# A long convolution's working tile: two channels of a place side by side, or eight

## The chip, the core and the metric

The kernel runs on one core of a Trainium2 chip. The core has five engines with a queue each: PE (TensorE) multiplies matrices, DVE (VectorE), ACT (ScalarE) and POOL (GpSimd) work on elements, and SP issues the DMAs. PE reads two operands from the on-chip memory: weights, which are loaded first (recorded as PEld, LDWEIGHTS), and a moving operand, which is then streamed past them (MATMUL). The metric is the time of one execution on the device in microseconds. Smaller is better.

## What is computed

A Hyena filter (a long convolution along the sequence, by FFT) is followed by a two-layer network on each token. Batch 4, sequence 12480, 128 channels, hidden width 2048:

```python
h_filt = (np.maximum(pos_emb @ w1, 0.0) @ w2) * np.exp(-0.01 * pos)[:, None]
u = x * v
Uf = np.fft.rfft(u, n=2*S, axis=1)
Hf = np.fft.rfft(h_filt, n=2*S, axis=0)
y = np.fft.irfft(Uf * Hf[None, :, :], n=2*S, axis=1)[:, :S, :]
a = (x * y).reshape(B * S, D)
h = a @ w_in
out = (h * np.cos(h)) @ w_out
```

All of it is float32.

## The kernel before

The transform of one sequence is split into two factors, N1 = 96 and N2 = 120, so that every step is a small matrix product. All steps of a batch work in place on one tile, `slots`. Its partitions are the positions of the factor that the next product sums over; along each partition it holds, before the change, 64 pairs of channels, for each pair 240 places, and for each place the two channels: `[P, 64, 240, 2]`. Two channels of a place thus lie side by side in 8 bytes, the next place of the same pair follows at once, and the same place of the next pair is 480 words (1920 bytes) further on.

A batch goes through these steps:

- **u**: x and v are loaded, multiplied (L437) and summed and subtracted into `slots` (`u_sums`, L447).
- **f1** (`f1_mm`, L455): for each pair of channels `b` and each of the two channels, two products with 64 and 60 rows of results. Here the tile is the *weights*: `u[:, b, lo:hi, i]`, one channel of 64 or 60 successive places, every second word. The table `c1` streams past it, 192 columns. The results go back to `slots` by a copy of ACT or DVE (`f1_evict`, L467), 384 words on end for each pair.
- **f2** (`f2_mm`, its products recorded at L136, the filter's at L488 and L491): for each frequency `k` the twiddled table `w` is the weights, and the tile is the *moving operand*: `parts[0:KE, :, k]`, the place `k` and its twin, of all channels, 256 columns in runs of two. The result is multiplied with the filter's spectrum `h` and put back (`f2_product`: DVE L508 and L510, POOL L511; in the first batch L504).
- **i1** (`i1_mm`, recorded at L136): as f1, with the tile as weights (96 places of one channel, 97 in the tiled part) and the table `cs` streaming, 120 columns. ACT and DVE put the results back (`i1_evict`: L531, L533; some by POOL, L527).
- **i2** (`i2_mm`, recorded at L136): for each output position the table `t` is the weights and a place of the tile is the moving operand, 128 columns in runs of two. The result is multiplied with x (L555) and stored.

The filter itself passes the same f1 and f2 once, through a tile of its own, `ftile`, and `above`, the last 48 places of `slots`. Its hidden layer lies in `aT`, a view of `above` (L387, L388), and is multiplied out by `filter_out` (L395, copies L401). While places of `slots` are free, the class `Between` lends them to the tables of sines and to five tiles of v.

The network takes the tokens in groups of 128 rows times four positions. For each group and each of 16 slices of the hidden width there is one product of 512 columns (`moe_up`, tile `ph`, later also `cv`), the cosine (L810, L811, L816, L817), sums for a Strassen scheme on POOL (L825 to L829), and a number of products of 128 columns (`moe_down`, L842, tiles `acca` and `accb`).

The order of work is written out by hand (`tc.manual_schedule`). A batch's steps are generators that yield a cost after each piece; the loop over the network's slices (98 groups of 16) lets them run for one unit of cost in each round (`convolve`), so the convolution of a batch is woven between the products of tokens that are already finished. Where the tokens run out, the convolution runs alone. From the network's start on `tiled[0]` is true: `mm` then cuts each product of the convolution and of `moe_up` into two column halves of PE (64 rows of results and the rest), which run together. The first batch's f1, f2 and i1 come before that and are not cut by `mm`; f1 cuts itself into 64 and 60 rows everywhere.

```python
    def mm(dst, left, right, start=True, stop=True):
        n = dst.shape[0]
        for lo, hi in ((0, CB), (CB, n)) if tiled[0] else ((0, n),):
            nc.tensor.matmul(dst[lo:hi], left[:, lo:hi], right, start=start, stop=stop)
```

Of the kernel before, what the change touches and what calls it, by code (L numbers as in the profile page):

```python
# [34 lines left out]
def kernel(  # L35
# [61 lines left out]
    FR = 2 * (2 * N2 - 2 * N1)  # L97
    KF = N1 - 2 * (N2 - N1)
    CB = D // 2
    assert R * N2 == S and S + TAPS - 1 <= 2 * M and math.exp(DECAY * TAPS) < 2.0 ** -150  # L100
    assert D == P and DFF % P == 0 and FO * 2 == P and N1 % 2 == 0 and R <= P
    assert NCH * ROWS <= FR <= R and H <= ODD and KE <= N1 + KF and H <= CB and N2 <= P
# [10 lines left out]
    WCOL = 256  # L113

    dram = ctx.enter_context(tc.tile_pool(name="dram", bufs=1, space=DRAM))
    hd = dram.tile([N1 // 2, N2, 2, CB, 4], F32, name="hd")
    zd = dram.tile([NROWS, G, D], F32, name="zd")
    wd = dram.tile([N1 // 2, KE, 2, N2], F32, name="wd")
    td = dram.tile([N2 // G, N1, G, 2, R], F32, name="td")
# [7 lines left out]
    c1 = const.tile([R, 3, N1], F32, name="c1")  # L127
    even = const.tile([KE, 2, N2], F32, name="even")
    tw_w = const.tile([KE, 2, N1], F32, name="tw_w")

    tiled = [False]

# [163 lines left out]
    class Between:  # L296


        def __init__(self, slots, first, last):
            self.places, self.used = slots[:, :, first:last, :], 0  # L300

        def tile(self, shape, dtype, name=None, bufs=1):
            n = 1 if len(shape) == 2 else shape[1]
            rows = self.places[0:shape[0], self.used:self.used + n].rearrange(
                "p b j i -> p b (j i)")[:, :, 0:shape[-1]]
            self.used += n
            return rows if len(shape) == 3 else rows[:, 0]

# [72 lines left out]
    def filter_hidden(bank, aT, i, peT, w1_sb):  # L381

        pa = bank()
        nc.tensor.matmul(pa[:, 0:ROWS * H], w1_sb[:, :], peT[:, :], start=True, stop=True)
        rows = slice(i * ROWS, (i + 1) * ROWS)
        pj = pa[:, 0:ROWS * H].rearrange("p (n a) -> p a n", a=H)
        nc.scalar.activation(aT[0:FO, 0:H, rows], pj[0:FO], AF.Relu)  # L387
        nc.vector.tensor_scalar(out=aT[FO:P, 0:H, rows], in0=pj[FO:P, ::-1, :],  # L388
                                scalar1=0.0, scalar2=None, op0=ALU.max)

    def filter_out(bank, aT, slots, j, w2_sb):

        ps = bank()
        for i, (jj, step) in enumerate(((H - 1 - j, 2), (j, 1))):
            nc.tensor.matmul(ps[0:FR, i * 2 * D:(i + 1) * 2 * D], aT[:, jj, 0:FR],  # L395
                             w2_sb[:, 0:step + 1:step, :], start=True, stop=True)
        pj = ps[0:FR, :].rearrange("p (n s b i) -> p s b n i", n=2, s=2, i=2)
        a = H - 2 - 2 * j
        for i in range(2):
            place = i * ODD + a  # L400
            nc.scalar.copy(out=slots[0:FR, :, place:place + 2, :], in_=pj[:, i])  # L401
# [37 lines left out]
    def u_sums(u, tiles, a, takers):  # L439
        both = tiles[0]  # L440
        if len(both.shape) == 4:
            both = both.rearrange("p h n (b i) -> p h n b i", i=2)
        else:
            both = both.rearrange("p h (n b i) -> p h n b i", n=UA, i=2)
        below, above = both[:, 0, ::-1, :, :], both[:, 1, :, :, :]
        for place, op, e in ((a, ALU.add, takers[0]), (ODD + a, ALU.subtract, takers[1])):
            e.tensor_tensor(u[0:R, :, place:place + UA, :].transpose([0, 2, 1, 3]),  # L447
                            below, above, op=op)


    def f1_mm(ps, u, b, i):

        dst = ps[:, i * 2 * N1:(i + 1) * 2 * N1]
        for r, (lo, hi) in enumerate(((0, ODD), (ODD, KE))):
            nc.tensor.matmul(dst[lo:hi], u[:, b, lo:hi, i],  # L455
                             c1[0:u.shape[0], r:r + 2, :].rearrange("p r k -> p (r k)"),
                             start=True, stop=True)

# [5 lines left out]

    def f1_evict(ps, b, share):
        pj = ps[:, 0:4 * N1].rearrange("p (i k) -> p k i", i=2)
        taker(b, share)(out=slots[0:KE, b, 0:2 * N1, :], in_=pj[0:KE])  # L467
        yield

    def f1_evict_filter(ps, b, share):  # L470

        pj = ps[:, 0:4 * N1].rearrange("p (i k) -> p k i", i=2)
        copy = taker(b, share)
        copy(out=ftile[0:KE, b, :, :], in_=pj[0:KE, 0:N1 + KF])
        yield
        copy(out=above[0:KE, b, :, :], in_=pj[0:KE, N1 + KF:])
        yield

    def f2_mm(ps, w, k1, i, filt=False):


        k = k1 + i
        pi = ps[0:N2, :].rearrange("p (r b g i) -> p g r b i", r=2, g=2, i=2)[:, i]
        if not filt:
            mm(pi, w[:, i, :], parts[0:KE, :, k])
        elif k < KF:
            both = ftile[0:KE, :, k:k + N1 + 1:N1, :].rearrange("p b r i -> p r b i")
            nc.tensor.matmul(pi, w[:, i, :], both, start=True, stop=True)  # L488
        else:
            for r, src in enumerate((ftile[0:KE, :, k, :], above[0:KE, :, k - KF, :])):  # L490
                nc.tensor.matmul(pi[:, r], w[:, i, :], src, start=True, stop=True)  # L491

    def f2_product(pool, ps, h, k1, whole, engine=nc.gpsimd):


        y = parts[0:N2, :, k1:k1 + 2, :, :].rearrange("p r k b i -> p r b (k i)")
        t = pool.tile([N2, 2, CB, 4], F32, name="t", bufs=2)
        uu = ps[0:N2, :].rearrange("p (r b j) -> p r b j", r=2, j=4)
        if whole:
            for r, (dst, hh) in enumerate(((y, h[:, :, :, :]), (t[:, :, :, :], h[:, ::-1, :, :]))):  # L500
# [12 lines left out]

    def i1_mm(ps, b, i):
        for r in range(2):
            n = max(N1, CB + CB // 2 + 1) if tiled[0] else N1
            mm(ps[0:n, (i * 2 + r) * N2:(i * 2 + r + 1) * N2],
               slots[0:N2, b, r * N1:r * N1 + n, i], cs[:, r, :])

    def i1_evict(pool, ps, b, apart):  # L520
        pj = ps[0:N1, 0:4 * N2].rearrange("p (i r j) -> p r j i", i=2, r=2)
        if apart:
            both = pool.tile([N1, 2, N2, 2], F32, name="both", bufs=1)
            nc.scalar.copy(out=both[:, :, :, :], in_=pj)
            yield
            for h, op in ((0, ALU.add), (1, ALU.subtract)):
                nc.gpsimd.tensor_tensor(slots[0:N1, b, h * N2:(h + 1) * N2, :], both[:, 0],  # L527
                                        both[:, 1], op=op)
            return
        other = pool.tile([N1, N2, 2], F32, name="other")  # L530
        nc.scalar.copy(out=other[:, :, :], in_=pj[:, 1])  # L531
        for h, op in ((0, ALU.add), (1, ALU.subtract)):
            nc.vector.tensor_tensor(slots[0:N1, b, h * N2:(h + 1) * N2, :], pj[:, 0],  # L533
                                    other[:, :, :], op=op)
            yield

# [103 lines left out]
    def f2_units(bank):  # L640
        with tc.tile_pool(name="there", bufs=3) as pool:
            ws, hs = {}, {}

            def before(j):
                ws[j] = pool.tile([KE, 2, N2], F32, name="w")
                nc.sync.dma_start(ws[j][:, :, :], wd[j, :, :, :])
                hs[j] = pool.tile([N2, 2, CB, 4], F32, name="h")
                nc.sync.dma_start(hs[j][:, :, :, :], hd[j, :, :, :, :])

            def mm(j, ps, i):  # L650
# [8 lines left out]
    def f2_both_units(bank):  # L659

        with tc.tile_pool(name="both", bufs=2) as pool:
# [15 lines left out]
                return ps  # L677

            def after(j, ps):
                h = pool.tile([N2, 2, CB, 4], F32, name="h", bufs=3)  # L680
# [209 lines left out]
    with tc.manual_schedule():  # L890
        with tc.tile_pool(name="psum", bufs=8, space=PSUM) as psum, \
# [8 lines left out]
            aT = above.rearrange("p b j i -> p b (j i)")  # L900


            keep = tc.tile_pool(name="keep", bufs=1)
# [1 line left out]
            with tc.tile_pool(name="layers", bufs=1, side="right") as pool:  # L905
# [34 lines left out]
                nc.gpsimd.memset(aT[:, 0:H, NCH * ROWS:FR], 0.0)  # L940
# [187 lines left out]
```

## Time and profile before

| | |
|---|---|
| median of 3 runs | 3674.19 us (3672.94 to 3674.47) |
| the profiled execution | 3673.78 us, of which the span from first to last instruction is 3671.2 us |
| granted TensorE clock, mean | 0.998 |
| first batch up to i1, nothing tiled | 0 to 303 us |
| i2 of the four batches | 303 to 530, 1139 to 1360, 2003 to 2224, 2889 to 3022 us |
| f1 of batches 2 to 4 (tiled) | 560 to 711, 1388 to 1536, 2252 to 2401 us |
| f2 of batches 2 to 4 (tiled) | 716 to 1042, 1543 to 1868, 2407 to 2732 us |
| i1 of batches 2 to 4 (tiled) | 1051 to 1138, 1877 to 2002, 2741 to 2884 us |
| the network alone | 3025 us to the end |

A profile line names the line of code, the engine, the operation, and the tiles written and read (`cv<-slots,w`: the bank `cv` is written from `slots` and `w`). `124*64` is the shape of the weights, `124x256` that of the moving operand. The number behind `x` counts records. A float32 matmul leaves two records of each kind, one for each of two passes. [...]

### The profile page before, as it was taken

Reading aid. Unit: us, or ns where it says so; the run is one execution under the profiler, and the core shown is the slowest. Engines: PE = TensorE matmul, PEld = TensorE weight load, DVE = VectorE, ACT = ScalarE, POOL = GpSimd, SP = SyncE. Lnnn points to the kernel's source line nnn. Section 1 sums busy time; section 2 is a strip of 40 time slices with the busy share of each in tenths; the row PEclk is TensorE's granted clock in tenths of the full one; section 3 lists DMA queues with packets and bytes.
Section 4 is the critical chain, followed back from the end, with each engine's and each line's share of the span. In section 5 each row is a group of like instructions: output and inputs, shape, how many; then the busy total and the mean of one; then the engine's idle time right before and its main releaser. Section 6 shows DMA issues by size and latency. Waiting matters only on the chain.

```text
span 3671.2 us, 101732 instructions
## 1 busy us (share of the span) xinstructions
PE 3605.1 (98%) x40810; PEld 2553.1 (70%) x40810; DVE 2811.3 (77%) x5289; ACT 2229.7 (61%) x4482; POOL 2757.7 (75%) x3237
## 2 busy tenths in 40 slices
PE   8999999999999999999999999999999999999999
PEld 6777776666678776666677776766667786666666
DVE  7777885688887776688887776578887667777777
ACT  6657666656554556655655556665555446666666
POOL 7667996688864886688874887578884448878877
PEclk9999999999999999999999999999999999999999
DMA  7454540022213551022211562012220350000000
GB/s 193 123 159 134 161 136 26 23 70 72 73 42 102 163 148 29 22 71 71 71 37 47 162 172 69 13 53 74 68 72 16 91 166 22 19 24 19 19 25 14
DMA packets 219583, 281.78 MB, mean 77 GB/s; under 512 B 18778, under 2 KB 156514, under 8 KB 218986
## 3 DMA queue, kind: packets, MB, share of 16 engines
q1 hardware_dynamic: 219114, 275.29, 26.3%
q8 instruction: 324, 5.31, 0.6%
q14 instruction: 145, 1.19, 0.1%
HBM read 194.75 MB, written 80.46 MB: 75 GB/s over the span
## 4 chain that ended last, share of the span: by engine, by line
PE 85%; DVE 4%; ACT 1%; POOL 1%; issue 1%; DMA 0%; ACTq 0%; DVEq 0%; POOLq 0%; SPq 0%
PE ph L136 30%; PE cv L136 18%; PE accb L842 17%; PE acca L842 13%; PE cv L455 3%; PE cv L140 1%; DVE gt L817 1%; DVE gt L811 1%; PE ph L140 1%; ACT gt L810 1%; POOL ts L825 0%; DVE t L510 0%; ACT tile L873 0%; DVE slots L508 0%; POOL ts L828 0%
## 5 line engine op out<-in xcount | busy, mean ns | idle before, releaser
L810 ACT ACTIVATE gt<-ph 128x512 int32<-128x512 f32 (+1 forms) x1380 | 823.1, 596 | 1143.4 <-PE ph L136 1087.6
L811 DVE SCALAR_TENSOR_TENSOR gt<-ph,gt 128x512 f32<-128x512 f32 (+1 forms) x1380 | 948.2, 687 | 716.0 <-ACT gt L810 712.9
L825 POOL TENSOR_TENSOR ts<-gt 128x512 f32<-128x512 f32 (+2 forms) x784 | 1006.2, 1283 | 581.8 <-PE accb L842 566.1
L136 PE MATMUL ph<-at,w_in_sb 128*64 128x512 f32 (+1 forms) x5520 | 1426.4, 592 | 13.3 <-ACT tile L873 6.8
L816 ACT ACTIVATE gt<-gt 128x512 f32<-128x512 f32 (+1 forms) x1568 | 972.0, 620 | 3.5 <-DVE gt L811 2.8
L817 DVE TENSOR_TENSOR gt<-ph,gt 128x512 f32<-128x512 f32 (+1 forms) x1380 | 934.7, 677 | 0.0
L842 PE MATMUL accb<-ts,w_out_sb 128*64 128x128 f32 (+2 forms) x9408 | 649.8, 272 | 0.0
L829 POOL TENSOR_TENSOR ts<-gt,ts 128x256 f32<-128x256 f32 (+2 forms) x784 | 574.4, 733 | 61.5
L828 POOL TENSOR_TENSOR ts<-ts,gt 128x256 f32<-128x256 f32 (+2 forms) x784 | 574.3, 732 | 61.5
L842 PEld LDWEIGHTS acca<-gt,w_out_sb 128*64 128x64 f32 x6272 | 398.9, 137 | 267.4 <-issue 231.3
L842 PEld LDWEIGHTS accb<-ts,w_out_sb 128*64 128x64 f32 x9408 | 543.5, 137 | 0.0
L842 PE MATMUL acca<-gt,w_out_sb 128*64 128x128 f32 (+2 forms) x6272 | 479.3, 272 | 0.0
L842 PEld LDWEIGHTS accb<-gt,w_out_sb 128*64 128x64 f32 x3136 | 225.5, 137 | 253.9 <-issue 198.8
L136 PEld LDWEIGHTS ph<-at,w_in_sb 128*64 128x64 f32 x5520 | 353.6, 137 | 32.8 <-ACT tile L873 15.0
L511 POOL TENSOR_TENSOR slots<-slots,t 120x256 f32<-120x256 f32 x383 | 280.7, 739 | 122.8 <-DVE t L510 70.2
L136 PEld LDWEIGHTS cv<-slots,tm 96*64 96x64 f32 (+1 forms) x3840 | 243.6, 127 | 119.6 <-issue 114.3
L842 PE MATMUL accb<-gt,w_out_sb 128*64 128x128 f32 (+1 forms) x3136 | 311.2, 273 | 4.2 <-DVE ot L863 2.8
L842 PE MATMUL acca<-ts,w_out_sb 128*64 128x128 f32 (+1 forms) x3136 | 308.7, 272 | 1.4 <-POOL ts L828 1.2
L136 PE MATMUL cv<-slots,tm 96*64 96x128 f32 (+1 forms) x3840 | 274.7, 285 | 3.9 <-DVE slots L533 3.4
L136 PEld LDWEIGHTS cv<-even,slots 120*64 120x64 f32 (+1 forms) x3072 | 168.4, 125 | 60.8 <-issue 58.8
L842 PEld LDWEIGHTS acca<-ts,w_out_sb 128*64 128x64 f32 x3136 | 201.6, 137 | 2.4 <-POOL ts L828 2.1
L136 PE MATMUL cv<-slots,w 124*64 124x256 f32 (+1 forms) x1152 | 191.1, 406 | 1.9 <-ACT at L799 1.9
(136 smaller groups left out, 3741.0 us busy)
## 6 DMA issues: line engine op xcount, KB each, us to landing
h<-hd SPq DMA_DIRECT2D x144, 240.0 KB
tm<-td SPq DMA_DIRECT2D x96, 312.0 KB
xt<-in_x_dram SPq DMA_DIRECT2D x120, 208.0 KB
xs<-in_x_dram SPq DMA_DIRECT2D x120, 208.0 KB
zd<-xs SPq DMA_DIRECT2D x119, 208.0 KB
tile<-zd SPq DMA_DIRECT2D x96, 256.0 KB
vt<-in_v_dram SPq DMA_DIRECT2D x90, 208.0 KB
w<-wd SPq DMA_DIRECT2D x144, 116.2 KB
```

What stands on the lines that cost most here:

```text
L136: nc.tensor.matmul(dst[lo:hi], left[:, lo:hi], right, start=start, stop=stop)
L140: nc.tensor.transpose(dst, src, ident[0:n, 0:n])
L455: nc.tensor.matmul(dst[lo:hi], u[:, b, lo:hi, i], c1[0:u.shape[0], r:r + 2, :].rearrange("p r k -> p (r k)"), start=True, stop=True)
L511: (engine if r else nc.gpsimd).tensor_tensor(y[:, r], y[:, r], t[:, r], op=op)
L810: nc.scalar.activation(turns, ph[:, 0:m], AF.Identity, bias=phase)
L811: nc.vector.scalar_tensor_tensor(out=part, in0=ph[:, 0:m], scalar=phase, in1=turns, op0=ALU.add, op1=ALU.subtract)
L816: nc.scalar.activation(part, part, AF.Sin, scale=scale)
L817: nc.vector.tensor_tensor(part, ph, part, op=ALU.mult)
L825: nc.gpsimd.tensor_tensor(ts[:, 0:2, 0:half], gt[:, :, half:2 * half], gt[:, 0, 0:2 * half].rearrange("p (h n) -> p h n", h=2), op=ALU.sub ...
L828: nc.gpsimd.tensor_tensor(t[2], t[1], b11, op=ALU.add)
L829: nc.gpsimd.tensor_tensor(t[3], b21, t[2], op=ALU.subtract)
L842: nc.tensor.matmul(acc[h * CB:(h + 1) * CB, place, 0:r], w_out_sb[:, pair, weight, :], right[:, h * r:(h + 1) * r], start=(pair == 0 and i ...
```

## The change

The tiles `slots`, `ftile`, the spectra `hd`, `h`, `t` and the view `aT` change their order along a partition. Instead of 64 pairs of channels there are 16 blocks of eight: `[P, 16, 240, 8]`. Eight channels of a place lie side by side in 32 bytes, the next place of the same channels is 8 words on, and the same place of the next block 1920 words (7680 bytes). The work is still done pair by pair where it was (`column` takes the two channels of a pair out of their block). So each access pattern changes its runs and steps: the moving operands of f2 and i2 have runs of eight in place of two; the weights of f1 and i1 take one word in eight in place of one in two; what f1 and i1 put back is written in pairs 32 bytes apart in place of one piece; u, the products of f2 and the filter's outputs are written in runs of eight or sixteen in place of two or four. The size of every tile stays, and so do the number and the kind of the instructions.

```diff
+    WIDE = 8
+    BLOCKS = D // WIDE
+    PAIRS = WIDE // 2
...
-    hd = dram.tile([N1 // 2, N2, 2, CB, 4], F32, name="hd")
+    hd = dram.tile([N1 // 2, N2, 2, BLOCKS, 2 * WIDE], F32, name="hd")
...
+    def column(t, b):
+        i = b % PAIRS * 2
+        return t[:, b // PAIRS, :, i:i + 2]
...
     def filter_out(bank, aT, slots, j, w2_sb):
-            nc.tensor.matmul(ps[0:FR, i * 2 * D:(i + 1) * 2 * D], aT[:, jj, 0:FR],
+            nc.tensor.matmul(ps[0:FR, i * 2 * D:(i + 1) * 2 * D], aT[:, jj // PAIRS, jj % PAIRS, 0:FR],
-        pj = ps[0:FR, :].rearrange("p (n s b i) -> p s b n i", n=2, s=2, i=2)
+        pj = ps[0:FR, :].rearrange("p (n s b i) -> p s b n i", n=2, s=2, i=WIDE)
...
     def u_sums(u, tiles, a, takers):
-            both = both.rearrange("p h n (b i) -> p h n b i", i=2)
+            both = both.rearrange("p h n (b i) -> p h n b i", i=WIDE)
...
     def f1_mm(ps, u, b, i):
-            nc.tensor.matmul(dst[lo:hi], u[:, b, lo:hi, i],
+            nc.tensor.matmul(dst[lo:hi], column(u, b)[:, lo:hi, i],
...
     def f1_evict(ps, b, share):
-        taker(b, share)(out=slots[0:KE, b, 0:2 * N1, :], in_=pj[0:KE])
+        taker(b, share)(out=column(slots, b)[0:KE, 0:2 * N1, :], in_=pj[0:KE])
...
     def f2_mm(ps, w, k1, i, filt=False):
-        pi = ps[0:N2, :].rearrange("p (r b g i) -> p g r b i", r=2, g=2, i=2)[:, i]
+        pi = ps[0:N2, :].rearrange("p (r b g i) -> p g r b i", r=2, g=2, i=WIDE)[:, i]
...
     def f2_product(pool, ps, h, k1, whole, engine=nc.gpsimd):
-        t = pool.tile([N2, 2, CB, 4], F32, name="t", bufs=2)
-        uu = ps[0:N2, :].rearrange("p (r b j) -> p r b j", r=2, j=4)
+        t = pool.tile([N2, 2, BLOCKS, 2 * WIDE], F32, name="t", bufs=2)
+        uu = ps[0:N2, :].rearrange("p (r b j) -> p r b j", r=2, j=2 * WIDE)
...
     def i1_mm(ps, b, i):
-               slots[0:N2, b, r * N1:r * N1 + n, i], cs[:, r, :])
+               column(slots, b)[0:N2, r * N1:r * N1 + n, i], cs[:, r, :])
...
     def i1_evict(pool, ps, b, apart):
-            nc.vector.tensor_tensor(slots[0:N1, b, h * N2:(h + 1) * N2, :], pj[:, 0],
+            nc.vector.tensor_tensor(column(slots, b)[0:N1, h * N2:(h + 1) * N2, :], pj[:, 0],
                                     other[:, :, :], op=op)
...
-            slots = spool.tile([P, CB, 2 * N2, 2], F32, name="slots")
+            slots = spool.tile([P, BLOCKS, 2 * N2, WIDE], F32, name="slots")
...
-            ftile = fpool.tile([P, CB, N1 + KF, 2], F32, name="ftile")
+            ftile = fpool.tile([P, BLOCKS, N1 + KF, WIDE], F32, name="ftile")
```

`Between` and the clearing of unused places are rewritten for the new order in the same way; they lend and clear the same number of words.

More of the change, by code (lines that the diff above doesn't have):

```diff
@@ L299, in __init__ @@
         def __init__(self, slots, first, last):
-            self.places, self.used = slots[:, :, first:last, :], 0
+            self.places, self.used = slots[:, :, first:last, :].rearrange(
+                "p b j i -> p b (j i)").rearrange("p b (q n) -> p b q n", q=PAIRS), 0
         def tile(self, shape, dtype, name=None, bufs=1):
             n = 1 if len(shape) == 2 else shape[1]
-            rows = self.places[0:shape[0], self.used:self.used + n].rearrange(
-                "p b j i -> p b (j i)")[:, :, 0:shape[-1]]
+            if self.used % PAIRS + n > PAIRS:
+                self.used += PAIRS - self.used % PAIRS
+            q = self.used % PAIRS
+            rows = self.places[0:shape[0], self.used // PAIRS, q:q + n, 0:shape[-1]]
             self.used += n
@@ L385, in filter_hidden @@
         rows = slice(i * ROWS, (i + 1) * ROWS)
-        pj = pa[:, 0:ROWS * H].rearrange("p (n a) -> p a n", a=H)
-        nc.scalar.activation(aT[0:FO, 0:H, rows], pj[0:FO], AF.Relu)
-        nc.vector.tensor_scalar(out=aT[FO:P, 0:H, rows], in0=pj[FO:P, ::-1, :],
+        pj = pa[:, 0:ROWS * H].rearrange("p (n b q) -> p b q n", b=H // PAIRS, q=PAIRS)
+        nc.scalar.activation(aT[0:FO, 0:H // PAIRS, :, rows], pj[0:FO], AF.Relu)
+        nc.vector.tensor_scalar(out=aT[FO:P, 0:H // PAIRS, :, rows], in0=pj[FO:P, ::-1, ::-1, :],
                                 scalar1=0.0, scalar2=None, op0=ALU.max)
@@ L441, in u_sums @@
         if len(both.shape) == 4:
-            both = both.rearrange("p h n (b i) -> p h n b i", i=2)
+            both = both.rearrange("p h n (b i) -> p h n b i", i=WIDE)
         else:
-            both = both.rearrange("p h (n b i) -> p h n b i", n=UA, i=2)
+            both = both.rearrange("p h (n b i) -> p h n b i", n=UA, i=WIDE)
         below, above = both[:, 0, ::-1, :, :], both[:, 1, :, :, :]
@@ L473, in f1_evict_filter @@
         copy = taker(b, share)
-        copy(out=ftile[0:KE, b, :, :], in_=pj[0:KE, 0:N1 + KF])
+        copy(out=column(ftile, b)[0:KE, :, :], in_=pj[0:KE, 0:N1 + KF])
         yield
-        copy(out=above[0:KE, b, :, :], in_=pj[0:KE, N1 + KF:])
+        copy(out=column(above, b)[0:KE, :, :], in_=pj[0:KE, N1 + KF:])
         yield
@@ L526, in i1_evict @@
             for h, op in ((0, ALU.add), (1, ALU.subtract)):
-                nc.gpsimd.tensor_tensor(slots[0:N1, b, h * N2:(h + 1) * N2, :], both[:, 0],
+                nc.gpsimd.tensor_tensor(column(slots, b)[0:N1, h * N2:(h + 1) * N2, :], both[:, 0],
                                         both[:, 1], op=op)
@@ L646, in before @@
                 nc.sync.dma_start(ws[j][:, :, :], wd[j, :, :, :])
-                hs[j] = pool.tile([N2, 2, CB, 4], F32, name="h")
+                hs[j] = pool.tile([N2, 2, BLOCKS, 2 * WIDE], F32, name="h")
                 nc.sync.dma_start(hs[j][:, :, :, :], hd[j, :, :, :, :])
@@ L679, in after @@
             def after(j, ps):
-                h = pool.tile([N2, 2, CB, 4], F32, name="h", bufs=3)
+                h = pool.tile([N2, 2, BLOCKS, 2 * WIDE], F32, name="h", bufs=3)
                 nc.scalar.activation(h[:, :, :, :].rearrange("p r b j -> p (r b j)"),
@@ L896 @@
             spool = ctx.enter_context(tc.tile_pool(name="slots", bufs=1))
-            slots = spool.tile([P, CB, 2 * N2, 2], F32, name="slots")
+            slots = spool.tile([P, BLOCKS, 2 * N2, WIDE], F32, name="slots")
             parts = slots[:, :, 0:2 * N1, :].rearrange("p b (r k) i -> p r k b i", r=2)
             above = slots[:, :, 2 * N1:2 * N2, :]
-            aT = above.rearrange("p b j i -> p b (j i)")
+            aT = above.rearrange("p b j i -> p b (j i)").rearrange(
+                "p b (q n) -> p b q n", q=PAIRS)
             keep = tc.tile_pool(name="keep", bufs=1)
@@ L939 @@
                 window = filter_window(pool)
-                nc.gpsimd.memset(aT[:, 0:H, NCH * ROWS:FR], 0.0)
+                nc.gpsimd.memset(aT[:, 0:H // PAIRS, :, NCH * ROWS:FR], 0.0)
                 sines = forward_tables(pool)
```

## The prediction

> **What bounds the kernel.** I read the page's busy shares and chain first, then a table by stage, then PE's timeline stage by stage.
>
> ```profile
> PE 3605.1 (98%) x40810; PEld 2553.1 (70%) x40810; DVE 2811.3 (77%) x5289; ACT 2229.7 (61%) x4482; POOL 2757.7 (75%) x3237
> ...
> PE 85%; DVE 4%; ACT 1%; POOL 1%; issue 1%; DMA 0%; ACTq 0%; DVEq 0%; POOLq 0%; SPq 0%
> ```
>
> PE (TensorE) is busy for 98% of the span and 85% of the chain that ends last. The table by stage (length; busy time of PE, weight loads, DVE, ACT, POOL; clock, DMA share, GB/s) agrees for the second batch's first step f1, its spectrum step f2, a stretch in which the inverse's first step i1 runs alone, and the last batch's output step i2:
>
> ```profile
> 560.00:716.00 156.00, 155.86 (x1754) 111.98 (x1755) 90.11 (x148) 102.33 (x208) 94.24 (x104) 1.00 0.08 22
> 716.00:1050.00 334.00, 329.69 (x3458) 212.47 (x3456) 287.05 (x567) 199.53 (x365) 292.22 (x343) 1.00 0.23 67
> 1106.00:1137.00 31.00, 31.00 (x606) 30.82 (x604) 26.70 (x76) 13.19 (x37) 1.25 (x2) 1.00 0.01 2
> 2887.00:3025.00 138.00, 138.00 (x1822) 110.89 (x1820) 82.83 (x136) 55.85 (x102) 64.88 (x71) 1.00 0.58 165
> ```
>
> PE is full and nothing else is, so PE's time here is nearly the span's. What counts is how fast it streams. A float32 matmul is recorded as two passes, and in the tiled part each pass as two column halves that run together: my unit is such a **pair** of records. The timeline gives start, busy time and count; a pair costs the distance to the next start, divided by the pairs.
>
> ```profile
> 989.69 1.03 PE L136 MATMUL ph<-at,w_in_sb 128*64 128x512 f32 x4
> 990.55 0.68 PE L136 MATMUL cv<-slots,w 124*64 124x256 f32 x4
> 991.07 0.61 PE L842 MATMUL acca<-gt,w_out_sb 128*64 128x128 f32 x8
> 991.51 0.39 PE L842 MATMUL acca<-ts,w_out_sb 128*64 128x128 f32 x4
> ...
> 994.32 0.64 PE L136 MATMUL cv<-slots,w 124*64 124x256 f32 x4
> 994.78 0.61 PE L842 MATMUL acca<-gt,w_out_sb 128*64 128x128 f32 x8
> ```
>
> The layer's products stream contiguous words: 0.86 us for two pairs of 512 columns is 0.84 ns a column (below: a **slot**); 0.44 us for four pairs of 128 columns is 110 ns a pair, 2.5 above 128 slots. f2 streams runs of two words: 0.52 and 0.46 us for two pairs of 256 columns, 245 ns a pair, where 256 slots and 2.5 are 217. i2 streams runs of two as well, 125 ns against 110:
>
> ```profile
> 2957.70 2.18 PE L136 MATMUL cv<-slots,tm 96*40 96x128 f32 x32
> 2959.70 0.63 PE L842 MATMUL acca<-gt,w_out_sb 128*64 128x128 f32 x8
> ```
>
> What slows them shows in f2's records, tiled (cv) and, in the first batch, as one full-width stream (ps); shortest/median/longest in ns:
>
> ```profile
> L136 PE MATMUL cv<-slots,w x1152: 376/414/470, 716.0 to 2731.9; 124*64 124x256 f32 x177, 124*56 124x256 f32 x15
> ...
> L136 PE MATMUL ps<-slots,w x192: 376/378/380, 146.2 to 242.2; 124*120 124x256 f32 x192
> ```
>
> One stream of two-word runs loses nothing, two lose up to 40 ns or more. Single records say when: of the tiled second-pass pairs, the 11 with no weight load beginning while they stream all last 376; the 235 with two loads have a median of 415. So PE's reads share something. The simplest count that fits is **one fetch per slot**: a run of two costs one fetch, so two such streams fill every slot, and the weight loads (64 and 56 columns) come on top. f2's excess is 28 ns, 33 slots for 120 weights, 0.28 of a fetch each; i2's is 15 ns, 18 slots for 104 weights, 0.17. A fetch would thus be some four contiguous words (0.25).
>
> **The change, part by part.** The two programs hold the same instructions with the same waits on PE, POOL and SP; on ACT two copies change places with conversions of the layer's weights, and one wait value of DVE differs by one. Only access patterns differ, so the sum is made of rates.
>
> *f2 and i2 on PE get runs of eight.* Two streams then need half a fetch per slot and leave room for the loads. f2: 245 - 217 = 28 ns x 576 pairs (1152 records) = 16 us. i2: 125 - 110 = 15 ns x 1920 pairs = 29 us. The bounds are nothing and these 45 us, contiguous speed, which a pattern cannot beat. I take 90%, 40 us, since in the stretches that also make the next u (303 to 560 us) POOL is busy for 223 us of 257 and PE waits now and then for it. The untiled f2 and the filter's gain nothing (376 to 378 already).
>
> *f1 and i1 on PE take their weights one word in eight* (32 bytes apart) where they took every second word. Today's step is free: i1 shows 32.39 us for 312 pairs,
>
> ```profile
> 1105.38 32.39 PE L136 MATMUL cv<-even,slots 120*64 120x120 f32 x624 [0.22 <-DVE slots L533]
> ```
>
> or 104 ns for 120 columns, 101 by slots and 2.5; f1 has 162.5 (four pairs in 0.65 us at 600.24) for 192 columns, by slots 161. By the count this is expected: i1's streams need 2 x 120/4 = 60 fetches and its 64 + 33 weights 49, 109 of 120 slots. After the change each weight is a fetch of its own: 60 + 97 = 157 slots = 132 ns, 28 more, x 1536 pairs = 43 us. f1: 2 x 192/4 + 64 + 60 = 220 slots = 185 ns, 22 more, x 768 pairs = 17 us. First batch: i1 is one stream, 30 + 96 = 126 slots = 106 ns, and takes 108 now (55.4 us for 512 records from 245.6 to 301.0): nothing. Its f1, filter and u, takes 190 and 175 ns a pair, waiting for evictions, so of 22 ns at most 10 show on 256 pairs: 2 us. Together 62 us. No row shows a weight read with a hop of over 8 bytes, so the bounds are wide: nothing, as for the hop of 8 bytes (a gain is excluded, since i1 and f1 already stream at a slot a column), and, if a lone word holds two slots, 60 + 194 = 254 slots = 213 ns for i1, 109 more, x 1536 = 167 us. I take 62, by the f2 rows, the nearest that show loads and streams collide.
>
> [...]
>
> *The copies into the tile* write pairs 32 bytes apart instead of one run: ACT (L467, 471 ns) and DVE (L533, 394 ns). The nearest row is POOL's L447, which writes pairs 1920 bytes apart: median 736 ns against 735 for the contiguous L829; DVE's L508 with runs of four takes 412 against 413 for L510, contiguous. So nothing, with an upper bound of 14 ns (L447's mean, 749) x 384 = 5 us. PE covers it: per block in i1 alone DVE needs 2 x 394 = 788 ns of PE's 830. Without that cover (PE at 100%, DVE above 415 each) it would show in full. *Runs of eight or sixteen in place of two or four* for L447, L508, L511 (739 ns) and ACT's L401 (369) save at most 14 ns each on engines that wait for PE: nothing, bounds 0 and 3 us. DMAs keep their pieces of 512 bytes.
>
> **Sum:** -40 + 62 = +22 us on the profiled execution's 3673.78 us (span 3671.2), which is 0.4 below the median shown: **3696 us**.
>
> **The rivals.**
> 1. *The lone weights are hidden, and the kernel is faster.* If a fetch is eight words rather than four (i2's 0.17 lies nearer to 1/8), i1 needs 30 + 97 = 127 slots, 107 ns, +3 x 1536 = 5 us, and f1 48 + 124 = 172, under its 192: nothing. Then -40 + 5 gives 3639. It decides from the point at which i1's pair stays within 104 ns. For it: a hop of 8 bytes costs nothing. Against it: f2's 0.28. Chance 0.33.
> 2. *In between:* a fetch of five words (the two rows' mean, 0.2) gives i1 48 + 97 = 145 slots, 122 ns, +18, 28 us; f1 77 + 124 = 201, 169, +6, 5 us; together -40 + 33, 3667 to 3681 with what else is uncertain. Chance 0.14.
> 3. *A lone word takes two slots even without competition.* The first batch's i1 loads 96 weights for 120 columns: 192 slots, 161 ns, +53 x 512 = 27 us, and the tiled f1 and i1 lie above my values as far as streams and loads collide: 3723 or more. No row speaks for it. [...] Chance 0.15.
> 4. *The change doesn't speed up the streams*, because what f2 and i2 lose lies in the loads or in PSUM, not in short runs: +62 alone, 3736. Against it: i2 writes PSUM in one run and loses too, and the layer's products, with the same loads and contiguous streams, lose nothing. Chance 0.05.
>
> The forecast has 0.33. The range runs from 3637 (rival 1, f2 and i2 gaining nearly all) to 3745 (rivals 3 and 4). By sign: faster 0.36 (rival 1 and some of 2), same 0.11, slower 0.53; 0.2%, 7 us, is about what a measurement of this kernel can tell from no change. Slower alone runs from 3682 to 3745.
>
> **What would show it.** f2's tiled pair at 217 to 220 ns and i2's at 110 to 112 show the gain right. i1's pair at some 130 and f1's at some 185 show the price; 104 and 162.5 mean rival 1; 161 in the untiled i1 means rival 3. L533 above 415 ns, or DVE full in the stretch of i1 alone, would mean that the copies, which I priced at nothing, are the bound. I am wrong if weight loads fetch in some other way than the streams do.

## The result, and the profile after

The changed kernel takes 3705.88 us (median of 4 runs, 3705.48 to 3707.76) where the kernel before takes 3673.6: a ratio of 1.0089, 95% interval 1.0071 to 1.0106. It is slower by 0.9%, 10 us above the forecast of 3696 and inside its range. The profiled execution's span is 3703.7 us, 32.5 longer than before, at the same mean granted clock (0.998).

The page's busy shares and the shares of the chain that ended last:

```profile
PE 3634.5 (98%) x40810; PEld 2654.3 (72%) x40810; DVE 2839.9 (77%) x5289; ACT 2239.3 (60%) x4482; POOL 2748.9 (74%) x3237
...
PE 82%; DVE 4%; ACT 1%; POOL 1%; issue 1%; DMA 0%; ACTq 0%; SPq 0%; POOLq 0%; DVEq 0%
```

The counts are those of before, PE is 98% busy again, and its busy time has grown by 29 us, that of the weight loads by 101. So the difference is again one of rates. The table by stage, for f1 and f2 of the second batch, the last batch's i2, and the first batch's i1 (which is not tiled):

```profile
593.60:751.50 157.90, 157.86 (x1754) 121.50 (x1756) 90.12 (x148) 104.42 (x208) 94.49 (x104) 0.99 0.08 22
751.50:1082.70 331.20, 326.35 (x3464) 212.07 (x3462) 287.27 (x569) 199.92 (x365) 292.07 (x344) 1.00 0.23 69
2922.50:3054.40 131.90, 131.90 (x1828) 105.88 (x1826) 82.99 (x138) 57.06 (x105) 63.75 (x71) 1.00 0.58 172
245.70:338.10 92.40, 92.40 (x512) 92.40 (x512) 39.53 (x111) 44.06 (x119) 33.50 (x50) 0.98 0.18 55
```

The same first i1 before:

```profile
245.60:301.00 55.40, 55.40 (x512) 55.40 (x512) 37.31 (x109) 41.11 (x119) 33.02 (x50) 0.95 0.30 92
```

The last row of the table against this one is the largest single piece of the difference: the same 512 records, alone on PE, take 92.4 us instead of 55.4. Each step's length from its first matmul to its last, in both traces, gives the whole account:

| step | before, us | after, us | difference |
|---|---|---|---|
| first batch's i1, untiled | 55.4 | 92.4 | +37.0 |
| i1 of batches 2 to 4 | 86.6, 124.4, 142.4 | 95.6, 133.1, 150.7 | +26.0 |
| f1 of batches 2 to 4 | 150.9, 148.9, 148.7 | 152.7, 149.1, 148.9 | +2.2 |
| f2 of batches 2 to 4 | 326.2, 325.2, 324.6 | 322.4, 321.5, 320.5 | -11.6 |
| i2 of the four batches | 227.3, 220.8, 220.7, 132.6 | 224.1, 215.4, 214.8, 126.2 | -20.9 |

The sum is +32.7 us, where the spans differ by 32.5. PE's timeline shows the new rates. They are read from the starts, since records overlap: f2's last 380 ns where its pairs start 217 apart, and those of the first i1 of before 266 where they start 103 apart. In the f2 stretch (start, busy time, count):

```profile
1025.79 1.03 PE L143 MATMUL ph<-at,w_in_sb 128*64 128x512 f32 x4
1026.65 0.60 PE L143 MATMUL cv<-slots,w 124*64 124x256 f32 x4
1027.08 0.61 PE L852 MATMUL acca<-gt,w_out_sb 128*64 128x128 f32 x8
```

Two pairs of f2 take 0.43 us, 215 ns a pair, against 0.52 and 0.46 us before: the speed of the layer's contiguous words, whose pairs of 512 columns take 0.86 us for two, 215 ns for 256 columns. i2 does the same, 16 records (8 pairs) in 0.87 us, 109 ns a pair:

```profile
2990.48 1.05 PE L143 MATMUL cv<-slots,tm 96*40 96x128 f32 x16
2991.35 0.40 PE L852 MATMUL accb<-gt,w_out_sb 128*64 128x128 f32 x4
```

f1, which takes its weights one word in eight now, has not changed its pace, 0.65 us for four pairs (the median of 185 such stretches is 652 ns in both traces):

```profile
640.11 0.82 PE L465 MATMUL cv<-c,slots 104*64 104x192 f32 x8
640.76 0.60 PE L852 MATMUL acca<-gt,w_out_sb 128*64 128x128 f32 x8
```

The groups by form (weights, moving operand, count; busy us, mean ns of one) show where the step is paid. Weight loads before, then after:

```profile
L455 PEld LDWEIGHTS cv<-c,slots 104*64 104x64 f32 x768 | 105.9, 139 | 105.9 <-issue 66.9 <-ACT slots L467 13.9 <-ACT gt L816 13.3
...
L136 PEld LDWEIGHTS cv<-even,slots 120*64 120x64 f32 x1536 | 165.1, 138 | 22.9 <-issue 21.0 <-ACT ot L856 1.8
...
L136 PEld LDWEIGHTS ps<-even,slots 120*96 120x96 f32 x512 | 55.5, 174 | 3.4 <-POOL slots L511 3.4
```

```profile
L465 PEld LDWEIGHTS cv<-c,slots 104*64 104x64 f32 x768 | 137.8, 197 | 75.9 <-issue 49.4 <-ACT slots L477 12.2 <-ACT gt L826 10.8
...
L143 PEld LDWEIGHTS cv<-even,slots 120*64 120x64 f32 x1536 | 204.6, 216 | 11.2 <-issue 5.9 <-ACT ot L866 1.1
...
L143 PEld LDWEIGHTS ps<-even,slots 120*96 120x96 f32 x512 | 92.5, 277 | 3.4 <-POOL slots L521 3.4
```

A load of 64 lone weights is recorded with 197 ns instead of 139, one of 96 with 277 instead of 174. f1's loads pay as i1's do, and f1 is not slower; so a dearer load does not by itself make a dearer product. In the untiled i1 the loads are busy without a gap (92.5 of 92.4 us): 180 ns between products, for 96 weights **1.88 ns a lone weight**, 2.2 slots of 0.84 ns.

### The profile page after: what moved, and what is told of

The parts are those of the page before. It is cut to its first block, busy times and chain, and to the rows that moved or that the text cites. A ratio compares the mean times of both kernels' runs of the same rounds, so it can differ in the third digit from the quotient of the medians.

```text
span 3703.7 us, 101732 instructions
## 1 busy us (share of the span) xinstructions
PE 3634.5 (98%) x40810; PEld 2654.3 (72%) x40810; DVE 2839.9 (77%) x5289; ACT 2239.3 (60%) x4482; POOL 2748.9 (74%) x3237
## 4 chain that ended last, share of the span: by engine, by line
PE 82%; DVE 4%; ACT 1%; POOL 1%; issue 1%; DMA 0%; ACTq 0%; SPq 0%; POOLq 0%; DVEq 0%
PE ph L143 30%; PE cv L143 17%; PE accb L852 17%; PE acca L852 13%; PE cv L465 3%; PE cv L147 1%; DVE gt L827 1%; DVE gt L821 1%; PE ph L147 1%; ACT gt L820 1%; POOL ts L835 0%; DVE t L520 0%; DMA vt<-in_v_dram 0%; DVE xt L447 0%; ACT tile L883 0%
## 5 line engine op out<-in xcount | busy, mean ns | idle before, releaser
L143 PE MATMUL ph<-at,w_in_sb 128*64 128x512 f32 (+1 forms) x5520 | 1442.3, 592 | 14.9 <-ACT tile L883 7.3
L852 PE MATMUL accb<-ts,w_out_sb 128*64 128x128 f32 (+2 forms) x9408 | 660.4, 272 | 0.0
L852 PE MATMUL acca<-gt,w_out_sb 128*64 128x128 f32 (+2 forms) x6272 | 489.9, 272 | 0.0
L143 PEld LDWEIGHTS ph<-at,w_in_sb 128*64 128x64 f32 x5520 | 362.8, 137 | 34.0 <-ACT tile L883 15.0
L521 POOL TENSOR_TENSOR slots<-slots,t 120x256 f32<-120x256 f32 x383 | 279.3, 736 | 114.7 <-DVE t L520 61.1
L852 PE MATMUL accb<-gt,w_out_sb 128*64 128x128 f32 (+1 forms) x3136 | 323.2, 274 | 4.4 <-DVE ot L873 3.2
L143 PEld LDWEIGHTS cv<-slots,tm 96*40 96x40 f32 (+1 forms) x3840 | 225.9, 127 | 118.7 <-issue 112.3
L143 PE MATMUL cv<-slots,tm 96*40 96x128 f32 (+1 forms) x3840 | 250.7, 273 | 4.1 <-DVE slots L543 3.2
L143 PEld LDWEIGHTS cv<-even,slots 120*33 120x33 f32 (+1 forms) x3072 | 231.1, 182 | 30.2 <-issue 6.7
L143 PE MATMUL cv<-even,slots 120*64 120x120 f32 (+1 forms) x3072 | 221.8, 282 | 0.0
L465 PEld LDWEIGHTS cv<-c,slots 104*64 104x64 f32 (+1 forms) x1536 | 140.9, 194 | 97.3 <-issue 69.8
```

What stands on the lines that cost most here:

```text
L465: nc.tensor.matmul(dst[lo:hi], column(u, b)[:, lo:hi, i], c1[0:u.shape[0], r:r + 2, :].rearrange("p r k -> p (r k)"), start=True, stop=True)
L852: nc.tensor.matmul(acc[h * CB:(h + 1) * CB, place, 0:r], w_out_sb[:, pair, weight, :], right[:, h * r:(h + 1) * r], start=(pair == 0 and i ...
```

## The experiments

Two theories were put against each other. **Own rate**: a lone weight (32 bytes to the next) holds the load that it belongs to for 1.88 ns; loads of different column parts run side by side, and a product takes the longer of its stream and its longest load. It gives 96 x 1.88 = 180 ns for the untiled i1, 64 x 1.88 = 120 for the tiled i1 (121 in the trace), and nothing for f1, since 120 is under its 162. **Count**, the prediction's: streams and loads share one fetch per slot, so what matters is the sum over both parts.

### Only the weights' step

```diff
 # in the kernel before, i1_mm
-               slots[0:N2, b, r * N1:r * N1 + n, i], cs[:, r, :])
+               flat[:, at:at + (n - 1) * 8 + 1:8], cs[:, r, :])
```

```diff
 # in the changed kernel, i1_mm
-               column(slots, b)[0:N2, r * N1:r * N1 + n, i], cs[:, r, :])
+               flat[:, at:at + 2 * n - 1:2], cs[:, r, :])
```

> The kernel before, in which only i1 takes its weights one word in eight (from places of three neighbouring pairs, so it computes with other words than it should; everything else is as before). This is the price of the change without its gain. Own rate: i1 at 180 ns in the first batch and 121 ns later, as in the changed kernel: +39 and +26 us on 3673.6, 3738. The shared count: first batch 126 slots = 106 ns, nothing, later 132 ns, 28 x 1536 = 43 us: 3717. If the price came from the layout of the writes or of the streams and not from the weights' step: 3674.

> The changed kernel, in which only i1 takes every second word again (words of the next block, so it computes with other words than it should). This is the gain without i1's price. Own rate: i1 at 104 ns in all batches, 65 us less than 3705.9: 3641. The shared count, by which f1 pays as well: i1's 43 us gone, f1's 17 stay: 3663 at the lowest. If the longer runs gained nothing: 3674 or more.

The step alone, in the kernel before, costs 76 us: 3750.48 us (3750.37 to 3755.69), ratio 1.0211 (1.0196 to 1.0226). The first i1 takes 95 us there, and those of the later batches 98, 136 and 153 us. That is 12 us above own rate. About half of it goes with waiting: the other words that i1 reads there are results of neighbouring pairs (the group of its first halves has 6.1 us of idle time, 0.4 before). Of the rest, 2.5 us lie in the first i1 (94.9, and 92.4 in the changed kernel) and 3.6 in i2 (804.9 us in all, and 801.3 before). Taken away from the changed kernel, it leaves 3641.32 us (3639.65 to 3643.06), ratio 0.9911 (0.9896 to 0.9925), the 3641 of own rate. Both halves of the change are thus measured apart: the runs of eight are worth 33 us, i1's lone weights cost 65 (3705.9 less 3641.3). f1's weights kept their step of eight words in this second kernel, and it lacks nothing of the gain: f1 pays nothing.

```diff
 # in the kernel before, i1_mm
+               flat[:, at:at + (n - 1) * 4 + 1:4], cs[:, r, :])
```

> The kernel before, with only i1's weights read one word in four (16 bytes apart) in place of every second word; i1 so reads other words than it should, and nothing else is changed. One word in eight gave 3750 (+76). [...]

3746.72 us (3745.08 to 3754.36), ratio 1.0199 (1.0184 to 1.0214): a step of four words costs about what a step of eight does, 72 us and 76, where a step of two leaves the first i1 at 55.4 us. The same price as at eight words would have been 3735 to 3751 us, one that grows with the bytes stepped over 3712 at most. So from four words to eight, twice the bytes, the price hardly grows; where between two words and four it begins was not shown, since a step of three was not run. In the first i1 the loads of 512 products with 96 weights are busy for 91.1 us at a step of four and, in the same kernel, 92.8 at a step of eight, 1.85 and 1.89 ns a weight; at a step of two words, 96 weights take at most the 103 ns between two products, 1.07 ns each.

### The same weights in other column parts

The price by own rate is set by the longest part, so cutting the product should remove it, with every weight still lone.

```diff
 # in the changed kernel, i1_mm, first batch only
+            edges = (0, CB, n) if tiled[0] else (0, CB // 2, CB, n)
+            for lo, hi in zip(edges, edges[1:]):
+                nc.tensor.matmul(dst[lo:hi], left[:, lo:hi], cs[:, r, :], start=True, stop=True)
```

> The changed kernel, with only the first batch's i1 (512 records, one product of 96 columns until now) cut into three column parts of 32, 32 and 32; later batches as in the changed kernel. Own rate (a lone weight holds its own load for 1.88 ns, and loads of different column parts run side by side): 32 weights x 1.88 = 60 ns are under the 101 ns of the stream, so i1 goes from 92.4 to about 56 us: 3706 - 36 = 3670 us. One shared count of fetches (120 columns x 3 parts in runs of four words, 90 slots, and 96 lone weights: 186 slots, 156 ns): 3706 - 12 = 3694. If the 92.4 us do not come from the weights: 3706.

3669.2 us (3666.24 to 3671.27), ratio to before 0.9985 (0.9975 to 0.9994). The first i1 is back at 54.5 us (245.2 to 299.7) with three loads of 32 lone weights side by side:

```profile
L531 PE MATMUL ps<-even,slots 120*32 120x120 f32 x1536 | 53.4, 266 | 3.2 <-DMA even<-csd 1.8 <-POOL slots L521 0.7 <-issue 0.6
L531 PEld LDWEIGHTS ps<-even,slots 120*32 120x32 f32 x1536 | 52.7, 138 | 4.1 <-POOL slots L521 3.2 <-issue 0.9
```

The count had 156 ns a product for this, 80 us; 53.4 us are 104 ns. This refutes a shared count. The second test changes only the size of the parts, in every batch; the second half's results go to rows 64 to 111:

```diff
 # in the changed kernel, i1_mm, all batches
+            for lo, at in ((0, 0), (N1 // 2, CB)):
+                nc.tensor.matmul(dst[at:at + N1 // 2], left[:, lo:lo + N1 // 2], cs[:, r, :],
+                                 start=True, stop=True)
```

> The changed kernel, with i1 of every batch in column halves of 48 and 48 weights (the second at rows 64 to 111 of the bank) in place of 64 and 33; the evictions then take the lower 48 rows only, so half of i1's result is left out; no instruction is added or taken away in the later batches. Own rate, where the larger part sets the time: 48 x 1.88 = 90 ns are under the 101 of the stream, so a pair takes 104 again in every batch: 3706 - 37 (first batch) - 26 (later ones) = 3643 us. One shared count: 60 + 96 lone weights, 156 slots, 131 ns: the first batch gains 512 x 49 = 25 us and the later ones nothing: 3681 or more.

3641.82 us (3641.48 to 3642.76), ratio 0.9914 (0.9899 to 0.9929). The products of 48 lone weights run as fast as those with a step of two words before:

```profile
L529 PE MATMUL cv<-even,slots 120*48 120x120 f32 x3072 | 179.8, 267 | 0.4 <-DVE slots L545 0.4
L529 PEld LDWEIGHTS cv<-even,slots 120*48 120x48 f32 x3072 | 174.1, 167 | 59.3 <-issue 53.6 <-ACT other L543 3.4 <-ACT ot L868 1.8
...
L529 PE MATMUL ps<-even,slots 120*48 120x120 f32 x1024 | 54.9, 271 | 2.6 <-DMA even<-csd 1.8 <-POOL slots L521 0.7
```

There are still 96 lone weights a product, and nothing is left of their price: by own rate a load of 48 takes 90 ns, less than the 104 between two products. And with the first batch in the later batches' parts, 64 and 33:

> The changed kernel, with the first batch's i1 cut into column halves of 64 and 33 (the later batches' cut) in place of 64 and 32, which ran one after the other. Own rate: 64 x 1.88 = 120 ns instead of 180, x 512 records = 31 us less than the changed kernel: 3675 us. One shared count of fetches: 60 + 97 = 157 slots, 132 ns: 3681. If two unequal parts never run side by side when nothing else is woven in: about 3910, as with 64 and 32.

3678.17 us (3675.9 to 3680.36), ratio 1.001 (1.0001 to 1.002), the first i1 at 64.7 us, 126 ns a product (own rate 120, count 132). That mean would not tell the two apart, but it holds a stretch with the granted clock at 0.57 (246 to 250 us) and some waits. A stretch without them does (length, busy times, clock, DMA share, GB/s):

```profile
260.00:300.00 40.00, 40.00 (x660) 40.00 (x657) 25.49 (x72) 27.82 (x81) 23.27 (x33) 1.00 0.14 43
```

It holds 330 pairs in 40 us, 121 ns each: own rate.

### Parts that do not run together

Two earlier runs were meant to show the same and came out 200 us and more above own rate. (The later batches' cut is 64 and 33, not 64 and 32 as the first expectation has it; that one column is what mattered.)

```diff
 # in the changed kernel, i1_mm: first batch 64 and 32
+            edges = (0, CB, n)
```

```diff
 # in the changed kernel, i1_mm: first batch 32, 32 and 32, later batches 32, 32 and 33
+            edges = (0, CB // 2, CB, n)
```

> The changed kernel, and in the first batch's i1 each product is cut into two column halves of 64 and 32 weights, as the later batches have it. Theory 'own rate' (formed from the changed kernel's trace: a weight that lies alone holds its own load for 180/96 = 1.88 ns, loads of different column halves run beside each other, and streams are not hurt): the product falls from 180 ns to 64 x 1.88 = 120 ns, 512 records x 60 ns = 31 us less than the changed kernel's 3705.9, so 3675. The count of the prediction (one fetch per slot, shared by streams and loads): two streams and 96 lone weights are 60 + 96 = 156 slots = 131 ns, 25 us less, 3681. If all lone weights share one reader: 180 ns as before, 3706.

> The changed kernel, and every product of i1 is cut into three column parts of 32, 32 and 32 or 33 weights. Own rate: the longest load is 33 x 1.88 = 62 ns, below the 104 ns that 120 columns stream, so i1 is at 104 ns again in all batches: (180 - 104) x 512 = 39 us and (121 - 104) x 1536 = 26 us less than 3705.9, so about 3641, faster than the kernel before by 0.9%. The shared count: three streams and 97 lone weights are 90 + 97 = 187 slots = 157 ns, 36 ns more than now x 1536 = 55 us, less 23 ns x 512 = 12 us: 3749. Third possibility, that no more than two column parts stream at a time: a third part adds a stream of its own, some 50 ns a product: about 3745 as well; the starts of the three parts would tell it from the shared count.

The first took 3910.37 us (3906.47 to 3911.46), ratio 1.0641 (1.0625 to 1.0657). Its parts of 64 and 32 ran one after the other, and the granted clock fell to 0.50 (length, busy times, then clock, DMA share and GB/s):

```profile
246.00:300.00 54.00, 53.43 (x186) 23.86 (x186) 7.98 (x21) 7.01 (x19) 4.82 (x9) 0.50 0.15 50
300.00:400.00 100.00, 100.00 (x349) 44.73 (x348) 13.66 (x38) 14.21 (x38) 13.81 (x18) 0.50 0.03 8
```

349 records in 100 us are 287 ns a record, 574 for the two parts, where two that ran side by side took 104 to 126. Twice that, an estimate for half the clock, is 252. In this i1 no two records start less than 186 ns apart, while in the run with 64 and 33 the second part starts some 33 ns after the first. The second took 4026.93 us (4025.23 to 4029.94), ratio 1.0959 (1.094 to 1.0977). Its first batch, three parts of 32, ran at the full rate (55.1 us), as own rate wants; its later ones, with a part of 33, did not, at a granted clock of 1.00. There the two parts of 32 start 7 ns apart, and the part of 33 starts 196 ns after them:

```profile
L531 PE MATMUL cv<-even,slots 120*32 120x120 f32 x3072 | 330.0, 293 | 0.0
L531 PE MATMUL cv<-even,slots 120*33 120x120 f32 x1536 | 326.3, 294 | 0.0
...
L531 PE MATMUL ps<-even,slots 120*32 120x120 f32 x1536 | 55.1, 271 | 3.1 <-DMA even<-csd 1.8 <-POOL slots L521 0.7 <-issue 0.5
```

64 with 33, 48 with 48 and 32 with 32 run together; 64 with 32 and 32 with 33 do not. So in these runs parts of 32 columns are one kind and parts of 33, 48 and 64 another, and PE did not run the two kinds at once in either run (no part under 32 was tried). Parts of 48 among the layer's parts of 64 lose nothing: with halves of 48, a stretch of eight pairs between two of the layer's products takes 0.83 us (1096.38 to 1097.21), 104 ns a pair. What does a change between kinds cost, when each product has one kind but its neighbours have another?

```diff
 # in the changed kernel, i1_mm, all batches, with n = 96
+            edges = (0, CB // 2, CB, n)
```

> The changed kernel, with i1 of every batch cut into three column parts of 32 (96 columns, where the later batches had 64 and 33). Own rate, if products of three parts and products of two parts (those of the layers, which are woven in) run into each other without loss: the first batch gives 36 us, the later ones 1536 pairs x (121 - 104) = 26: 3706 - 62 = 3644 us. If parts of 32 and parts of 64 in one stretch wait for each other, as the 64 and 32 of one product did in the run with halves: the loss is at every change between them; i1's stretches have some 30 changes per 100 us, and at 0.1 to 1 us each that is 10 to 100 us over all, so 3655 to 3745, and i1's stretches show it: gaps beside the layers' products and not inside i1's own. If unequal parts had nothing to do with the serial stretches of the run with three parts (32, 32, 33): about 4000 again.

3674.69 us (3673.58 to 3677.16), ratio 1.0001 (0.9991 to 1.001): the 62 us are halved. PE's timeline shows the rest at the changes:

```profile
1046.80 0.64 PE L531 MATMUL cv<-even,slots 120*32 120x120 f32 x12
1047.37 0.66 PE L855 MATMUL acca<-gt,w_out_sb 128*64 128x128 f32 x8
1047.86 0.39 PE L855 MATMUL acca<-ts,w_out_sb 128*64 128x128 f32 x4
1048.08 1.03 PE L143 MATMUL ph<-at,w_in_sb 128*64 128x512 f32 x4
1049.04 1.05 PE L531 MATMUL cv<-even,slots 120*32 120x120 f32 x24
```

Stretches of 12, 24 and 36 records (4, 8 and 12 times three parts) take 571, 982 and 1392 ns: 103 ns each and 160 ns at the end. The 0.96 us of the layer's product ahead of i1 are 0.10 above its 0.86. Together 0.26 us for each of 115 stretches, 30 us of the 31 that are missing. The price of a change there and back is 0.26 us at the ends of such a stretch.

The two kinds give a version: thirds in the first batch and in the two stretches where i1 is alone, 64 and 33 elsewhere. The second line sets the first pair of channels that is cut in thirds, for each later batch in turn.

```diff
 # in the changed kernel: i1_mm, and ahead of each later batch
+            edges = (0, CB // 2, CB, N1) if b >= thirds[0] else (0, CB, CB + CB // 2 + 1)
...
+                    thirds[0] = (24, 51, CB)[b]
```

> The changed kernel, with i1 in three column parts of 32 in the first batch and in the two stretches of the later batches in which nothing is woven in between (320 of 512 pairs of the second batch, 104 of the third), and in 64 and 33 elsewhere. From the runs with thirds: in those stretches a pair takes 112 and 114 ns with thirds, 126 and 135 with halves: 320 x 14 + 104 x 21 = 6.7 us less than the run with thirds in the first batch alone (3669), with at most 1 us lost at the few changes between thirds and halves: 3663 us. If that run's loss was spread over i1 itself and not at the changes: 3669 or more.

3661.44 us (3660.64 to 3664.49), ratio to before 0.9969 (0.9958 to 0.9979): faster than both kernels, and 0.3% faster than the kernel before.

### Does one stream of short runs lose?

```diff
 # in the kernel before, f2_mm and i2_mm
-            mm(pi, w[:, i, :], parts[0:KE, :, k])
+            nc.tensor.matmul(pi, w[:, i, :], parts[0:KE, :, k], start=True, stop=True)
...
-                mm(ps[0:R, i * D:(i + 1) * D], t[:, i, r, :], slots[0:N1, :, place, :],
-                   start=(r == 0), stop=(r == 1))
+                nc.tensor.matmul(ps[0:R, i * D:(i + 1) * D], t[:, i, r, :], slots[0:N1, :, place, :],
+                                 start=(r == 0), stop=(r == 1))
```

> The kernel before, with f2 and i2 of the later batches each as one full-width product instead of two column halves (runs of two words as in before; nothing else changed). If runs of two lose only because two streams read at once: inside a stretch i2 falls from 123 to 110 ns a pass and f2 from 246 to 218, 41 us over all, 3633 without a loss at the changes between full width and halves; there are some 290 such stretches of f2 and 220 of i2, and at the 0.26 us that a change cost with three parts they add 130 us: 3765. If a stream of two-word runs loses by itself: 123 and 246 stay inside the stretches.

3785.95 us (3784.21 to 3787.24), ratio 1.0306 (1.029 to 1.0321). Inside the stretches the first forecast holds. i2's timeline, and f2's record (shortest, median, longest ns):

```profile
2996.48 1.13 PE L548 MATMUL cv<-slots,tm 96*104 96x128 f32 x8
2997.54 0.66 PE L842 MATMUL acca<-gt,w_out_sb 128*64 128x128 f32 x8
```

```profile
L485 PE MATMUL cv<-slots,w x576: 375/379/481, 724.9 to 2836.0; 124*120 124x256 f32 x192
```

f2's record has a median of 379 ns, where the two halves had 414, and inside a stretch i2's records start 110 ns apart, where pairs took 123. So it does take two streams to lose. The 8 records of i2 last 1.06 us, 0.18 more than 8 x 110, and the whole kernel loses 112 us where 41 should have been won: 153 us at 507 stretches, 0.30 us each. That is near the 0.26 of the thirds, and it lies at the changes there too.

## Why the prediction was right or wrong

The sign and the time were right, 3706 against 3696, but by terms of which four were off and largely cancelled: with f1 17 us too dear, the tiled i1 17 too dear, the untiled i1 37 too cheap and the gain 7 too high, +22 becomes the +32 that was measured. That the sum came so near is luck: the one count behind all the terms of the price is refuted. Its four words to a fetch were an estimate from f2's excess that no run shows: f1 stayed at 163 ns a pair where it gave 185, and the tiled i1 went to 121 where it gave 132.

- **The bound** was right: PE is full in both kernels, and the times are rates on PE.
- **f2 and i2, -40**: -32.5, by the stages and by the kernel with only this half of the change (3641). The rates are those foreseen, 215 to 218 and 109 ns. The term was too large because the rates before were read from single stretches, 245 and 125; the medians of all stretches are 483 ns for two pairs and 980 for eight, 241.5 and 122.5. That gives 24 x 576 + 13 x 1920 = 39 us; the missing 6 lie in f2 and in the i2 of the first three batches, most in the first (3.2 of 6.2 us), while the last batch's i2, which makes no u, got all of its 6.2.
- **The tiled i1, +43**: +26. The price is there but follows another rule: 64 x 1.88 ns, the longer half alone, not 157 fetches of both. Rival 2 had this place right (122 ns, +28) by accident: it adds loads to streams too, which gave f1 169 ns, where 163 were measured, and the first batch's i1 nothing.
- **f1, +17 and +2**: +2 in all, and not from the weights. This is the step that failed in its mechanism: the count of 2 x 192/4 + 64 + 60 = 220 slots adds the loads of both halves to their streams. The runs with 32 and with 48 weights a part show that they do not add. Of the 2.2 us, 1.8 lie in the second batch, whose f1 began with the granted clock at 0.57:

```profile
593.60:597.60 4.00, 3.96 (x25) 3.27 (x27) 0.00 (x0) 0.00 (x0) 3.84 (x5) 0.57 0.39 102
```

  In the kernel before with only i1's step changed, whose f1 is the old one, the clock had the same 0.57 from 601 to 605 us, and that f1 took 152.6 us, as the changed one's 152.7.
- **The first batch's i1, nothing**: +37, the largest term of the result. The count gave 126 slots and so 106 ns; in truth 96 weights in one load are 180. This is the mechanism of rival 3, whose bound for this place was 27, from two slots a lone weight, which no row of before shows; the run shows 2.2 (180 ns for 96); that rival's conclusion, 3723 or more, fell with its second half, that the tiled products would suffer more than by the count.
- **Copies and the other engines, nothing**: right for DVE (L543 395 ns, 394 before) and POOL (L521 736, 739 before). ACT's copy, which I priced at nothing too, costs 36 ns more (before, then after):

```profile
L467 ACT COPY slots<-cv x192: 470/471/496, 563.9 to 2403.8; 124x384 f32<-124x384 f32 x192
...
L477 ACT COPY slots<-cv x192: 498/507/532, 599.2 to 2438.7; 124x384 f32<-124x384 f32 x192
```

It is 192 x 36 = 7 us of ACT, under PE: f1's 2 us are nearly all the clock's, so it does not show.

What stays open: why two streams of two-word runs lose 11 to 12% while one loses nothing. Runs of eight and a single stream both end it. That loads collide with streams, as the prediction had it, was not shown; the 11 pairs without a load speak for it, though one of them lasts 420 ns and not 376, but no run took the loads away. Open too is why the clock stayed at 0.50 with 64 and 32 and not with 32, 32 and 33.

## What to carry to other kernels

Price a layout at every reader apart: for each product compare the stream's time with the longest single weight load. In these runs a strided load cost nothing where it stayed the shorter (64 x 1.88 = 120 ns under f1's 163, 48 x 1.88 = 90 under i1's 104). A step of two float32 words left i1 at 103 ns, one of four or eight made it 1.85 to 1.89 ns a weight, and a cut into more equal column parts took the first i1 from 180 back to 104 ns; where the neighbours on PE were of the other kind, a stretch lost 0.26 us. Where a sum rests on one rule that no row shows at work, give most care to the place where the rivals differ most: here the first batch's i1, 96 weights in one load against 120 columns, priced at nothing, was the largest term.

## What the runs showed of the hardware

- A product of 96 float32 weights in one load and 120 columns takes 180 ns (median from start to start) with the weights at a step of eight words and 103 at a step of two; at a step of four its loads alone are busy for 178 ns (91.1 us for 512). In parts of 48 or 32 weights it takes 104 at a step of eight as well (32.54 us for 312 pairs; 53.4 us for 512 products).
- A column part of 32 did not run at once with one of 64 or of 33: 64 with 32 took 287 ns a record at clock 0.50, 574 for both, while 64 with 33 took 121 to 126 ns for both; 32, 32 and 33 took 356 ns for the three at clock 1.00 (674 records in 80 us), where 32, 32 and 32 took 104.
- A stretch of products of another part size cost 0.26 us (32 among 64) to 0.30 us (full width among 64), at its two ends together.
- PE's granted clock was 0.50 while its records left no gap: the serial parts of 64 and 32 filled 100 of 100 us (300 to 400 us). With 32, 32 and 33 the two kinds also ran one after the other, and it was 1.00 (1180 to 1260 us).
- ACT's write in pairs 32 bytes apart took 507 ns where one contiguous piece took 471; DVE's took 395 and 394.
